# Attention scores of six chunks in 64x64 tiles of the array, with K loaded in interleaved groups of 64 tokens

## Chip, core and metric

The kernel runs on one core of a Trainium2 chip. The metric is the device time of one execution in microseconds (us). Its engines are named as in the profile: PE is TensorE (matmuls), PEld its weight loads, DVE is VectorE, ACT is ScalarE, POOL is GpSimd, and SP is SyncE, which here only issues DMAs.

## What is computed

Attention with 4 sink tokens and a sliding window of 128 tokens, for 4 batches, 8 heads, 768 tokens and a head size of 64, and then a feed-forward layer whose hidden value is the maximum of three products:

```python
scores = scale * np.matmul(q, k.transpose(0, 1, 3, 2))
is_sink = pos[None, :] < n_sink
rel = pos[:, None] - pos[None, :]
keep = is_sink | ((rel >= 0) & (rel < window))
scores = np.where(keep, scores, -1000000000.0)
a = np.exp(scores - max); a = a / (a.sum() + 1e-09)
x = np.matmul(a, v)          # heads side by side: 3072 tokens x 512
h = np.maximum(np.maximum(x @ w1, x @ w2), x @ w3)
out = h @ w_out
```

Inputs and output are float32; the kernel computes in bf16 with float32 sums.

## The kernel before

The tokens are cut into 12 chunks of 256, three to a batch (`CPB` = 3). A chunk has two blocks of 128 queries and two of 128 keys. Partitions hold pairs of tokens: in a load (`load`, L76) partition p holds tokens 2p and 2p+1 of the chunk, so a block n of 128 keys is on 64 partitions, with the two tokens of a pair (index i) side by side.

A chunk goes through these steps. POOL casts K, Q and V to bf16 (`cast_qk` L102, `cast_v` L108). For chunks 4 to 11 K and Q are turned by DMA transposes that SP issues (`turn_dma`, L153), K in two transposes of 64 partitions, Q in one. PE computes the scores of a pair of heads p (`score`, L272). The two heads (index a) of the pair are on partitions 0 to 63 and 64 to 127, so each matmul uses 64 rows of the array and all of its 128 columns. A chunk that is not the first of its batch has four score blocks of 128 keys by 128 queries: slot 0 is the block of the chunk before against the first queries, slots 1 and 2 the chunk's first keys against both query blocks, and slot 3 its second keys against the second queries. In each block a triangle lies outside the window, but all 128x128 are computed. ACT takes the exponential of a full PSUM bank per head (`expo`, L335), DVE multiplies by a mask of ones and zeros (`mask`, L341), and PE multiplies by V (`av`, L398) into four banks that `av_open` (L381) has started with the sink tokens. A first chunk of a batch (3, 6, 9) has three blocks per pair of heads and no sink part. From chunk 6 on these are packed into three sets of four (`score_packed` L307, `expo_packed` L318, `mask_packed` L323 with the mask `mskp`, which ACT copies from `msk0` during chunk 3, L221 to L224). The result x is turned by a DMA transpose (`xpose_dma`, L425), and PE runs the feed-forward layer: `ffn_h` (L438, nine groups of eight matmuls for a chunk, maxima on DVE at L449, first product copied by ACT at L445) and `ffn_y` (L459, twelve matmuls, copied out by DVE or ACT, L461).

All of this stands in an order that is written out by hand: each engine executes its instructions in the order of the program. From L715 on a loop runs over stages i = 3 to 11; stage i has the attention of chunk n = i + 1, the hidden layer of chunk i, the output layer of chunk m = i - 1, and loads, casts and transposes for chunk i + 3. In a stage the scores of pairs 0, 3 and 1 come first, then the twelve matmuls of `ffn_y`, then the scores of pair 2, and then `av` and `ffn_h` in turns. PSUM has eight banks; `bank` (L57) takes the bank that was given back longest ago and makes a new tile in it.

## Time and profile before

| | us |
|---|---|
| time, median of 3 runs | 177.45 (177.33 to 177.59) |
| the profiled execution | 177.2 |
| its span, first to last instruction | 175.4 |
| PE busy | 168.9 (96%), 1872 matmuls |
| DVE busy | 123.5 (70%) |
| ACT busy | 88.8 (51%) |
| POOL busy | 66.9 (38%) |

The profile is one execution. Its page gives busy times, a chain of waits (the work that ended last, followed back from the end) and groups of instructions by source line. Other views of the same trace are quoted with their filters named in words: a timeline gives start and duration in us, then engine, line, operation, tiles and, in brackets, the idle time before it and what ended it. Matmul ends are modelled, so a busy PE is not a PE at its peak, and start times say more than durations.

### The profile page before, as it was taken

How to read it: one execution, taken by the hardware profiler on the slowest of the kernel's cores; microseconds unless marked ns; L12 is line 12 of the kernel's file. 1: busy time of each engine (PE TensorE's matmuls, PEld its weight loads, DVE VectorE, ACT ScalarE, POOL GpSimd, SP SyncE). 2: the span in 40 equal slices, each digit the busy share in tenths (PEclk: the TensorE clock that was granted, in tenths of full speed). 3: DMA queues.
4: the chain of work that ended last, by engine and by line, in shares of the span. 5: the costliest groups of instructions: out<-in, count | busy, mean ns of one | idle time of the engine just before them, and what ended most of it. 6: DMA issues, size and time to landing. Idle time of an engine off the chain costs nothing.

```text
span 175.4 us, 4631 instructions
## 1 busy us (share of the span) xinstructions
PE 168.9 (96%) x1872; PEld 127.1 (72%) x1872; DVE 123.5 (70%) x264; ACT 88.8 (51%) x173; POOL 66.9 (38%) x123
## 2 busy tenths in 40 slices
PE   6989999999999999999999999999999999999991
PEld 2446889856896697697796796796895895896870
DVE  3389828599698496895875975877775775976460
ACT  3398741586995823814716715715517617510211
POOL 6785335046480555734735328038246000000000
PEclk9999999999999999999999999999999999999999
DMA  4999999994999989899999999999999429223203
GB/s 134 291 289 205 215 259 254 216 278 124 297 168 237 107 214 238 168 294 150 214 305 162 260 278 149 274 247 142 274 271 125 149 51 398 95 54 129 120 2 120
DMA packets 69573, 34.90 MB, mean 199 GB/s; under 512 B 26544, under 2 KB 68016, under 8 KB 69552
## 3 DMA queue, kind: packets, MB, share of 16 engines
q1 hardware_dynamic: 64912, 31.33, 80.0%
q0 software_dynamic: 4496, 3.15, 11.8%
q8 instruction: 14, 0.23, 0.6%
q10 hardware_dynamic: 144, 0.13, 0.2%
q14 instruction: 7, 0.06, 0.1%
HBM read 25.17 MB, written 6.29 MB: 179 GB/s over the span
## 4 chain that ended last, share of the span: by engine, by line
PE 90%; DMA 4%; SPq 2%; POOL 1%; issue 0%; DVE 0%; ACT 0%; POOLq 0%
PE h_ps L438 54%; PE y_ps L459 18%; PE o L398 6%; PE st L287 6%; DMA q_raw<-in_q_dram 4%; SPq L90 2%; PE xt L419 1%; PE o L381 1%; PE pt L118 1%; PE sk L349 1%; PE st L307 1%; PE y_ps L469 1%; POOL q_bf L102 1%; PE st L269 0%; PE pt L140 0%
## 5 line engine op out<-in xcount | busy, mean ns | idle before, releaser
L438 PE MATMUL h_ps<-xT,w 128*128 128x256 bf16 x864 | 100.4, 273 | 0.0
L438 PEld LDWEIGHTS <-w 128*128 128x128 bf16 x864 | 82.2, 98 | 10.2 <-issue 0.5
L449 DVE TENSOR_TENSOR h_sb<-h_sb,h_ps 128x512 bf16<-128x512 bf16 (+1 forms) x74 | 49.2, 671 | 20.3 <-PE h_ps L438 19.1
L445 ACT CAST h_sb<-h_ps 128x512 bf16<-128x512 f32 x36 | 21.2, 590 | 42.9 <-PE h_ps L438 42.9
L335 ACT ACTIVATE e_sb<-st 128x512 bf16<-128x512 f32 (+1 forms) x80 | 40.2, 593 | 1.0 <-PE st L287 0.8
L108 POOL CAST vb<-v_raw 64x512 bf16<-64x512 f32 x38 | 27.4, 722 | 15.6 <-DMA v_raw<-in_v_dram 10.7
L459 PE MATMUL y_ps<-wo,h_sb 128*128 128x512 bf16 x138 | 32.2, 380 | 0.0
L341 DVE TENSOR_TENSOR e_sb<-e_sb,msk 128x1024 bf16<-128x1024 bf16 (+1 forms) x34 | 24.9, 765 | 3.5 <-ACT e_sb L335 3.3
L459 PEld LDWEIGHTS <-h_sb 128*128 128x128 bf16 x138 | 12.6, 98 | 14.8 <-issue 1.2
L406 DVE TENSOR_TENSOR x_sb<-o,rc 128x256 bf16<-128x256 f32 x48 | 20.4, 425 | 1.7
L102 POOL CAST k_bf<-k_raw 128x512 bf16<-128x512 f32 x17 | 10.3, 625 | 28.5 <-DMA k_raw<-in_k_dram 25.8
L102 POOL CAST q_bf<-q_raw 128x512 bf16<-128x512 f32 x21 | 13.3, 659 | 14.9 <-DMA q_raw<-in_q_dram 11.4
L461 DVE COPY y_sb<-y_ps 128x512 f32<-128x512 f32 x13 | 9.0, 690 | 10.9 <-PE y_ps L459 10.8
L398 PE MATMUL o<-vb,e_sb 128*128 128x65 bf16 x352 | 16.4, 193 | 0.0
L398 PEld LDWEIGHTS <-e_sb 128*128 128x128 bf16 x352 | 14.6, 97 | 2.3
L287 PE MATMUL st<-qT,kT 64*128 64x128 bf16 (+1 forms) x224 | 12.5, 237 | 0.5 <-ACT kT L125 0.5
L287 PEld LDWEIGHTS <-kT 64*128 64x128 bf16 x224 | 7.1, 94 | 6.0 <-issue 3.8
L355 ACT ACTIVATE e_sink<-sk 128x256 bf16<-128x256 f32 x8 | 3.1, 386 | 15.0 <-PE sk L349 10.5
L403 DVE RECIPROCAL rc<-o 128x4 f32<-128x4 f32 x48 | 8.4, 176 | 3.2 <-PE o L398 3.1
L318 ACT ACTIVATE e_sb<-st 128x512 bf16<-128x512 f32 x12 | 6.1, 613 | 4.7 <-PE st L307 4.7
L461 ACT COPY y_sb<-y_ps 128x512 f32<-128x512 f32 x10 | 5.9, 588 | 2.1 <-PE y_ps L459 1.6
L102 ACT CAST k_bf<-k_raw 128x512 bf16<-128x512 f32 x5 | 3.1, 627 | 6.7 <-DMA k_raw<-in_k_dram 6.7
(78 smaller groups left out, 87.6 us busy)
## 6 DMA issues: line engine op xcount, KB each, us to landing
k_raw<-in_k_dram SPq DMA_DIRECT2D x12, 512.0 KB, 5.7
q_raw<-in_q_dram SPq DMA_DIRECT2D x12, 512.0 KB, 6.8
v_raw<-in_v_dram SPq DMA_DIRECT2D x12, 512.0 KB, 8.1
out_dram<-y_sb SPq DMA_DIRECT2D x11, 512.0 KB, 4.1
w<-in_moe_w_dram POOLq DMA_DIRECT2D x5, 256.0 KB, 8.6
w<-in_moe_w_dram POOLq DMA_DIRECT2D x2, 512.0 KB, 9.8
wo<-in_moe_w_out_dram POOLq DMA_DIRECT2D x2, 384.0 KB, 9.7
kT<-k_bf SPq DMA_TRANSPOSE x16, 3.5
```

The source lines that it names most:

```text
L102: f(x[:, 2 * g:2 * g + 2].rearrange("q p i a d -> q p a i d"), y[:, 4 * g:4 * g + 4].rearrange("q (p a) i d -> q p a i d", a=2))
L108: (eng.copy if eng is nc.scalar else eng.tensor_copy)(vb[ci % RING][64 * i:64 * i + 64, n, :, 0:D], raws[ci, "v"][64 * n:64 * n + 64, :, i])
L287: nc.tensor.matmul(st[a][:, s:s + q1 - q0].rearrange("q n (i r) -> q n i r", i=2), lhsT=x[hp, n, p].rearrange("q i r -> q (i r)"), rhs=qc[ ...
L335: nc.scalar.activation(e[:, a, lo:], st[a][:, lo:], AF.Exp, scale=scale)
L341: (eng or nc.vector).tensor_mul(e[:, :, lo:], e[:, :, lo:], msk0 if lo else msk)
L398: nc.tensor.matmul(o[:, t, a], lhsT=weight(ci, p, a, s), rhs=vb[cv % RING][:, n, 2 * p + a], start=first, stop=True, skip_group_check=True)
L406: nc.vector.tensor_mul(xs[ci][:, :, p], o[:, :, :, 0:D], rc.unsqueeze(3).to_broadcast([128, 2, 2, D]))
L438: nc.tensor.matmul(hp[:, f].rearrange("q (i t r) -> q i t r", i=2, t=2), lhsT=w_sb[wi][:, ds, c0:c0 + 128], rhs=xTs[ci][:, :, ds].rearrang ...
L445: nc.scalar.copy(dst, hp)
L449: nc.vector.tensor_max(dst[:, x], dst[:, x], hp[:, x])
L459: nc.tensor.matmul(yp, lhsT=hs[ci][:, fb, t * 128:(t + 1) * 128], rhs=wo[:, fb], start=(fb == 0), stop=(fb == FB - 1))
L461: (nc.scalar.copy if eng is None else eng.tensor_copy)(ys[ci][:, t], yp)
```

## The change

For chunks 6 to 11 (`SKEW` = 6) the 256 tokens of K and V are no longer taken as two blocks of 128 but as four groups g of 64 keys.

- K is loaded by four DMAs, one for each group, each onto every fourth partition (group g on partitions g, g+4, ...). After one transpose of all 128 partitions, the keys of a group stand four elements apart, and the matmul reads 64 of them as weights with a stride of four (`groups`).
- `score_skew` replaces `score`: 16 matmuls for a pair of heads instead of 6, each on 64 rows and 64 columns of the array (`tile_position=(64 * a, 64 * h)`, h = g % 2). Per head and column half it streams 128, 128, 64 and 64 query columns, where `score` streamed 128, 256 and 128 through all columns. Parts of the bank that no query needs are not written, and hold what was there before.
- `score_packed` of chunks 6 and 9 gives each of its matmuls to two 64-column tiles, with the same query columns: 32 matmuls instead of 16.
- Since the exponential may now read anything in the unwritten parts, the mask is a minimum with 0 or a very large number (`mskg`, `mskg0`, `mskp`) instead of a product. `mskg` is made by POOL behind K's cast for chunk 2; `mskg0` by POOL, and from it `mskp` by ACT, in stage 4 (the attention of chunk 5).
- V follows the groups' partition order: eight casts of 32 partitions instead of four of 64.
- `bank` makes eight tiles once and hands out views of them. Matmuls no longer wait on PE's own semaphore when a bank is taken again (93 such waits before); ACT's and DVE's reads of a bank name both PE and the other reader.

The core of the diff:

```diff
+        BANK = [psum.tile([128, 512], F32, name=f"bank{j}") for j in range(8)]
         def bank(shape, dtype, name):
             j = free.pop(0)
-            x = psum.tile(shape, dtype, tag=f"b{j}", name=name)
+            x = BANK[j][:, 0:n] if dtype is F32 else BANK[j][:, 0:n // 2].bitcast(dtype)
...
+        def groups(ci):
+            return kT[ci % RING].rearrange("q n p i r -> q (n p i r)").rearrange(
+                "q (p x g) -> q p x g", p=NP, g=4)
...
+                if w == "k" and ci >= SKEW:
+                    for g in range(4):
+                        nc.sync.dma_start(
+                            out=dst[g:128:4],
+                            in_=src[b, :, t0 + 64 * g:t0 + 64 * g + 64].rearrange("h (p i) d -> p h (i d)", i=2))
+                    continue
...
+            for h in range(2):
+                f(vb[ci % RING][64 * h + 32 * i:64 * h + 32 * i + 32, n, :, 0:D],
+                  raws[ci, "v"][64 * n + 32 * h:64 * n + 32 * h + 32, :, i])
...
+            if ci >= SKEW:
+                nc.sync.dma_start_transpose(
+                    out=groups(ci).rearrange("q p (i u) g -> q (p i) (u g)", i=2),
+                    in_=bfs[ci, w].rearrange("s p i a d -> s (p i a d)"))
+                return
...
+        def score_skew(ci, pairs):
+            k0, k1 = groups(ci - 1), groups(ci)
+            plan = ((1, k1, 0, 0, None), (2, k1, 1, 1, None), (3, k1, 2, 1, None), (0, k0, 3, 0, None),
+                    (2, k1, 0, 1, 0), (1, k1, 1, 0, 1), (0, k0, 2, 0, 0), (3, k1, 3, 1, 1))
+            for p in pairs:
+                st = [bank([128, 4, 128], F32, "st") for a in range(2)]
+                for s, x, g, t, u in plan:
+                    h = g % 2
+                    r = slice(0, 64) if u is None else slice(32 * u, 32 * u + 32)
+                    for a in range(2):
+                        hp = slice(64 * a, 64 * a + 64)
+                        nc.tensor.matmul(
+                            st[a][64 * h:64 * h + 64, s].rearrange("q (i r) -> q i r", i=2)[:, :, r],
+                            lhsT=x[hp, p, :, g],
+                            rhs=qT[ci % RING][hp, p, :, t, r],
+                            start=True, stop=True, tile_position=(64 * a, 64 * h))
...
-            nc.vector.tensor_mul(e, e, mskp[:, j // 2])
+            nc.vector.tensor_tensor(out=e, in0=e, in1=mskp[:, j // 2], op=ALU.min)
...
+                masks_skew(2) if i == 4 else None
...
+                masks_packed() if i == 4 else None
```

The order of instructions at three places. First PE, at the scores of the first pair of heads of chunk 8; `kT0` holds chunk 8's keys and `kT3` chunk 7's. Before, the whole pair:

```order
L287 LDWEIGHTS kT3_72
L287 MATMUL st_2102<-qT0_73,kT3_72 128x128
L287 LDWEIGHTS kT3_72
L287 MATMUL st_2103<-qT0_73,kT3_72 128x128
L287 LDWEIGHTS kT0_69
L287 MATMUL st_2102<-qT0_73,kT0_69 128x256
L287 LDWEIGHTS kT0_69
L287 MATMUL st_2103<-qT0_73,kT0_69 128x256
L287 LDWEIGHTS kT0_69
L287 MATMUL st_2102<-qT0_73,kT0_69 128x128
L287 LDWEIGHTS kT0_69
L287 MATMUL st_2103<-qT0_73,kT0_69 128x128
```

The middle of the same pair after the change, the second half of the long matmuls' last round and the first round of short ones:

```order
L348 LDWEIGHTS kT3_80
L348 MATMUL bank5_74<-qT0_81,kT3_80 64x128
L348 LDWEIGHTS kT3_80
L348 MATMUL bank2_71<-qT0_81,kT3_80 64x128
L348 LDWEIGHTS kT0_77
L348 MATMUL bank5_74<-qT0_81,kT0_77 64x2x32
L348 LDWEIGHTS kT0_77
L348 MATMUL bank2_71<-qT0_81,kT0_77 64x2x32
L348 LDWEIGHTS kT0_77
L348 MATMUL bank5_74<-qT0_81,kT0_77 64x2x32
L348 LDWEIGHTS kT0_77
L348 MATMUL bank2_71<-qT0_81,kT0_77 64x2x32
```

Three pairs of a weight load and a matmul per head have become eight, still with the two heads in turn, and four matmuls in a row now fall on four different tiles.

Second POOL, from the casts for chunk 6 to those for chunk 7 (`vb_87` and `vb_79` are chunk 6's V, `mskg_111` is `mskg0`). Before:

```order
L102 CAST q_bf<-q_raw 128x2x2x2x64 x2
L108 CAST vb_79<-v_raw 64x8x64 x4
L102 CAST k_bf<-k_raw 128x2x2x2x64 x2
L102 CAST q_bf<-q_raw 128x2x2x2x64 x2
L108 CAST vb_80<-v_raw 64x8x64 x4
L242 COPY ks_81<-kT_71 64x4x4 x2
```

After:

```order
L122 CAST q_bf<-q_raw 128x2x2x2x64 x2
L134 CAST vb_87<-v_raw 32x8x64 x8
L275 COPY mskg_111<-mskg 128x384
L277 MEMSET mskg_111 2x256 x2
L275 COPY mskg_111<-mskg 128x384
L277 MEMSET mskg_111 2x256 x2
L122 CAST k_bf<-k_raw 128x2x2x2x64 x2
L122 CAST q_bf<-q_raw 128x2x2x2x64 x2
L134 CAST vb_88<-v_raw 32x8x64 x8
L306 COPY ks_89<-kT_79 64x4x4 x2
```

V's casts have doubled, and six instructions for `mskg0` have come in ahead of chunk 7's casts.

Third ACT, between the hidden layer of stage 4 and the exponentials of chunk 6. Before, these stood behind one another:

```order
L445 CAST h_sb<-h_ps 128x512 x3
L318 ACTIVATE e_sb<-st 128x512 x6
L461 COPY y_sb<-y_ps 128x512
L445 CAST h_sb<-h_ps 128x512 x3
L355 ACTIVATE e_sink<-sk 128x256
```

After:

```order
L535 CAST h_sb<-bank_71 128x512
L283 COPY mskp<-mskg_111 128x2x384
L284 COPY mskp<-mskg_111 128x2x128
L286 COPY mskp<-mskg_111 128x2x256 x2
L405 ACTIVATE e_sb<-bank_70 128x512
L405 ACTIVATE e_sb<-bank_73 128x512
```

The four copies that make `mskp` have moved here from chunk 3's stage, and the first of them waits for POOL's `mskg0`.

83 lines of the change are left out of this document (66 added, 17 removed).

## Prediction

> **What bounds the kernel now.** I read the busy times first, then the chain of waits, by line and then in order of time.
>
> ```profile
> PE 168.9 (96%) x1872; PEld 127.1 (72%) x1872; DVE 123.5 (70%) x264; ACT 88.8 (51%) x173; POOL 66.9 (38%) x123
> PE 90%; DMA 4%; SPq 2%; POOL 1%; issue 0%; DVE 0%; ACT 0%; POOLq 0%
> ```
>
> PE's 96% alone proves little, since matmul ends are modelled. The chain says more: 90% of it is PE, unbroken but for 0.03 us from 13.60 us (the first row below) to the last output copy. There PE waits for nobody, so a nanosecond taken from its instructions is a nanosecond of the kernel, and work on other engines costs nothing until it makes PE wait. The stage with the attention of chunk 8 shows what a chunk's scores cost, and the rest that I need:
>
> ```profile
> 13.60 0.40 PE pt L140 x4
> ...
> 106.77 0.22 PE sk L349 x4
> 107.00 0.77 PE st L287 x18
> 107.77 2.70 PE y_ps L459 x12
> 110.46 0.33 PE st L287 x6
> 110.79 0.22 PE o L381 x8
> 111.01 0.35 PE o L398 x8
> 115.58 4.37 PE h_ps L438 x40
> 119.95 0.77 PE st L307 x16
> ```
>
> Three pairs of heads take 0.77 us and one takes 0.33, so a pair costs 0.22 and going into and out of the tiled mode 0.11. A matmul of `ffn_h` with 256 columns takes 4.37 / 40 = 0.109 us. A pair of heads streams 512 columns for each of two heads; at that pace one head alone is 0.218 us. So the two row halves of the array run side by side, and the scores are bound by streamed columns. The changed scores cost PE 4 x 1.10 = 4.4 us in chunks 7, 8, 10 and 11, and 2 x 0.77 in the packed chunks 6 and 9: the change works on 6 of 177 us.
>
> **The full chunks' scores.** A column half of a head now streams 128 + 128 + 64 + 64 = 384 columns. If all four tiles run side by side, as the two row halves do, a pair loses 128 columns, 128 x 0.109 / 256 = 0.055 us, and 16 pairs lose 0.87 us. Whether column tiles overlap and reload behind one another is shown by the sink rows, which use four tiles of 32 columns:
>
> ```profile
> 57.27 0.25 PE L365 MATMUL sv<-vb,sel 128*32 128x65 bf16 x8
> 57.34 0.28 PE L349 MATMUL sk<-qT,ks 128*32 128x256 bf16 x4
> 57.56 0.61 PE L459 MATMUL y_ps<-wo,h_sb 128*128 128x512 bf16 x2
> L349 PE MATMUL sk<-qT,ks x16: 270/283/283, 57.3 to 106.7; 128*32 128x256 bf16 x16
> ```
>
> Eight matmuls of 65 columns, each with weights of its own, pass in 0.07 us, two rounds of four; one after another they would need 8 x 65 x 0.109 / 256 = 0.22. So four column tiles overlap, and the second round's weights arrive within a round of 65 columns. The weights of the changed scores have 64 columns and a stride of four; no row has either. Between bounds of 0 (no gain, if each short round waits for its weights as long as a long one lasts) and -0.87 I take the whole -0.87, because the nearest rows are at that end.
>
> The first weights after a change of mode can't hide. In the last row the shortest of 16 matmuls (270 ns, the case in which other sink matmuls ran ahead) and the usual one (283) differ by 13 ns, which I read as one exposed load of 32 columns. Twice the columns make it 13 ns more, at eight entries in full chunks and two in packed ones: +0.13 us.
>
> **The packed chunks.** 32 matmuls for 16, with the same columns for each tile: 0 if the tiles overlap.
>
> Here the Trainium skill speaks against the change. Its page "TensorEngine Tiling (Array Packing)" (Restrictions and Gotchas) says that column tiling excludes the fast weight load, and "TensorE: Matmul & The Clock Gate" (LDWEIGHTS) puts a plain load at columns / 1.2 ns, which would be an estimated 53 ns for 64 columns, as long as a 128-column round; a pair would then save next to nothing. The 13 ns above for 32 columns is half of what that rule gives (27 ns), so I side with the row and keep the rule's result as a rival.
>
> **DVE, POOL and DMA, hidden.** The minimum takes the place of a product with the same operands, types and shape; no row has a minimum out of SBUF, I take 0, and the maximum of L449 bounds it from above (686 ns for half the elements, 0.6 us more per mask).
>
> V's casts double, since a cast costs by its row length:
>
> ```profile
> L108 POOL CAST vb<-v_raw 64x512 bf16<-64x512 f32 x38 | 27.4, 722 | 15.6 <-DMA v_raw<-in_v_dram 10.7 <-PE st L307 2.3 <-PE st L287 0.7
> 71.13 3.67 POOL L108 CAST vb<-v_raw 64x512 bf16<-64x512 f32 x4 [1.86 <-DMA v_raw<-in_v_dram]
> 77.09 1.17 POOL L102 CAST k_bf<-k_raw 128x512 bf16<-128x512 f32 x2 [2.30 <-DMA k_raw<-in_k_dram]
> 103.06 1.17 POOL L102 CAST k_bf<-k_raw 128x512 bf16<-128x512 f32 x2 [5.13 <-DMA k_raw<-in_k_dram]
> ```
>
> Four more at 0.72 are 2.9 us in a stage of 13 us, in which POOL idles 2 to 5 us ahead of the next K cast alone. Longer casts meet DVE's masks, which slow down beside POOL, but that has been paid already in chunk 5:
>
> ```profile
> 71.23 3.08 DVE L341 TENSOR_TENSOR e_sb<-e_sb,msk 128x1024 bf16<-128x1024 bf16 x3
> 109.81 1.92 DVE L341 TENSOR_TENSOR e_sb<-e_sb,msk 128x1024 bf16<-128x1024 bf16 x3
> 68.19:81.38 13.19, 13.19 (x154) 9.93 (x156) 10.30 (x19) 6.69 (x13) 6.92 (x10) 1.00 1.22 206
> 106.77:119.95 13.18, 13.18 (x155) 9.99 (x156) 9.31 (x19) 6.69 (x13) 4.97 (x9) 1.00 1.03 229
> ```
>
> Three masks took 3.08 us beside casts and 1.92 without, and the two stages are 13.19 and 13.18 us long: 0. K's four DMAs for one and one transpose for two change landing times by a microsecond or so, behind which q and v loads queue on SP; chunk 9's K, cast at 103.06, is first multiplied at 119.95, so 0, as long as the delay stays far below 10 us. The masks made early stand on POOL ahead of chunk 2's V casts:
>
> ```profile
> L198 POOL TENSOR_SCALAR_AFFINE_SELECT addm<-addm 64x128 bf16<-64x128 bf16 x2 | 0.6, 294 | 0.1
> 34.94 0.61 POOL L108 CAST vb<-v_raw 64x512 bf16<-64x512 f32 x1 [4.81 <-DMA v_raw<-in_v_dram]
> ```
>
> A memset, eight selects at 0.29 and a few copies are some 4 us, in the 4.81 in which POOL waits for that V: 0. The bank views take 93 waits of PE on itself away; forty matmuls of `ffn_h` in a row, with five new banks, already run at the 0.109 us of their columns, so there is nothing in them to gain: 0.
>
> **One place is tight: `mskp` for chunk 6.**
>
> ```profile
> L215 POOL TENSOR_SCALAR msk<-addm 128x384 bf16<-128x384 bf16 x2 | 1.1, 538 | 0.1
> L195 POOL MEMSET addm<- 128x256 bf16 x1 | 0.3, 318 | 0.0
> L221 ACT COPY mskp<-msk 128x768 bf16<-128x768 bf16 x1 | 0.8, 833 | 0.0
> L224 ACT COPY mskp<-msk 128x512 bf16<-128x512 bf16 x2 | 1.1, 616 | 0.0
> L222 ACT COPY mskp<-msk 128x256 bf16<-128x256 bf16 x1 | 0.4, 401 | 0.0
> 78.80 0.59 ACT L445 CAST h_sb<-h_ps 128x512 bf16<-128x512 f32 x1 [3.65 <-PE h_ps L438]
> 81.74 3.05 ACT L318 ACTIVATE e_sb<-st 128x512 bf16<-128x512 f32 x6 [2.36 <-PE st L307]
> 82.86 0.69 DVE L323 TENSOR_TENSOR e_sb<-e_sb,mskp 128x1024 bf16<-128x1024 bf16 x1 [0.75 <-ACT e_sb L318]
> 84.84 0.18 PE o L398 x6
> ```
>
> Chunk 6's V casts end at 74.8 now; four more end at 77.8. `mskg0` is two copies like L215 and four memsets like L195, 2.3 us: 80.1. ACT's copies are 0.83 + 0.40 + 2 x 0.62 = 2.5 us: 82.6, where the exponentials began at 81.74. They, and the six queued behind (DVE's first packed mask waits for them, and the copy of y behind it), start 0.9 us late; the mask, over at 83.55, ends at 84.4, and PE wants it at 84.7 to 84.8. That fits by 0.3 us. If K's four DMAs bring V a microsecond later, PE waits 0.7. I take 0.15.
>
> **Sum.** -0.87 + 0.13 + 0.15 = -0.59 us. The profiled execution is 177.2, so 176.6; the median of 177.45 is 0.25 above it, so **176.9** beside the runs.
>
> **Rivals.** *Slower: PE gets its instructions too slowly.* A load and its matmul go by every 0.22 / 6 = 37 ns now, and would have to every 10 ns.
>
> ```profile
> 17.84 0.22 PE o L381 x8
> 18.06 0.88 PE o L398 x24
> L307 PEldq EVENT_SEMAPHORE  x2: 51/51/51, 79.3 to 117.8; - x2
> ```
>
> The densest long stretch of the trace has 32 in 1.10 us, 34 ns each. PE's sequencer runs ahead: its wait for L307 stands at 117.8, 2 us before the first of these matmuls, so about 2 / 0.109 = 18 are ready. Of three pairs of heads, 48, some 30 come at 34 ns: 1.02 us for 0.66 in each of four chunks, +1.44; the last pair still saves 0.055 x 4, and 32 packed ones fit. With the 0.28 above this is +1.5, **179.0**. It turns against the change when a pair comes slower than 0.66 / 30 = 22 ns. Against it: 12 sink pairs in 0.29 us (57.27 to 57.56), though these fit into what is ready. The Trainium skill's "Runtime: NRT & Kernel Launch" (Instruction fetch mechanics) gives some 20 cycles for an instruction, an estimated 33 ns for a load and matmul; no run here shows it.
>
> *No gain: weights of 64 columns with a stride take as long as 128 streamed columns.* A pair stays at 0.22, and 0.28 is left: **177.7**.
>
> *The column halves don't overlap.* 768 columns for a pair, 0.33 us: +0.11 x 16 + 2 x 0.66 + 0.28 = +3.3, **180.8**; the sink rows speak against it.
>
> *Chunk 6 waits for its mask by 0.7 us:* **177.4**.
>
> **Chances.** Forecast 0.54 (176.5 to 177.2), instructions too slow 0.21, weights too slow 0.13, late mask 0.06, halves in turn 0.06. A difference under 0.2% (0.35 us) can't be told from none here. Faster 0.50, all of the forecast but its upper end; same 0.17 (0.04 of the forecast, 0.09 of the weights, 0.04 of the mask); slower 0.33. The range goes from 176.4, all of the columns' gain and no wait, to 179.1, which takes in the instruction case; the halves in turn are left out.
>
> **What would show it.** Eighteen changed score matmuls became 48: their piece of the chain in chunk 8 should fall from 0.77 to about 0.63 us, and the last pair's from 0.33 to 0.29. Pieces over 0.8 speak for slow instructions, of about 0.77 for slow weights, near 1.1 with packed pieces doubled for halves in turn. In chunk 6 no wait of PE on DVE should exceed 0.3 us. The stages of chunks 1 to 5 should keep their lengths; if they don't, the bank views did something that I cost at nothing.

## The result, and the profile after

The changed kernel takes 179.29 us (median of 4 runs, 179.19 to 179.50) against 177.52 us for the kernel before (4 runs), a ratio of 1.0101, 95% interval [1.0084, 1.0119]: slower by 1.0%. The forecast of 176.9 us was wrong, and its range ended at 179.1. Measured again (experiment 5) the ratio was 1.0076 [1.0054, 1.0098]. Beside experiments 1 to 4 the executions of the kernel before spread from 177.06 to 178.80 us, so one execution proves little, and the experiments below count more than one profile. Executions more than 1.5% above the fastest of their kernel are left out of the ratios but not of the medians, so the two need not agree.

In the page after, PE's share of the span is the same 96%, but its share of the chain has fallen from 90% to 87%, and DVE has come in with 5%. DMA's 4% was a load of the start-up; its 3% is now a transpose of x in the middle of the kernel:

```profile
PE 169.6 (96%) x2052; PEld 129.5 (73%) x2064; DVE 124.6 (70%) x264; ACT 88.7 (50%) x173; POOL 92.1 (52%) x167
...
PE 87%; DVE 5%; DMA 3%; issue 1%; ACT 1%; POOL 1%; POOLq 0%; DVEq 0%; ACTq 0%
```

PE's tiles are all named `bank` now, and lines have moved: `score_skew` is L348, `score_packed` L394, `ffn_h` L528. In the chain of waits of the changed kernel (start, us, what) the scores of chunk 8 and of the packed chunk 9 are longer than before, not shorter (0.77, 0.33 and 0.77; where a row has x15 for 16 matmuls, a record is missing from the trace):

```profile
108.89 0.85 PE bank L348 x48
...
112.44 0.37 PE bank L348 x15
...
121.97 0.83 PE bank L394 x32
```

A pair of heads takes (0.85 - 0.37) / 2 = 0.24 us where 0.22 stood and 0.165 was forecast. Further up, the same chain leaves PE in stage 4 for the transposed x and in chunk 6 for its mask (and once more ahead of both, along DVE from 36.3 to 40.5 us; experiment 13 comes back to that):

```profile
68.25 5.87 DMA xT<-x_sb
...
74.16 1.91 PE bank L528 x16
...
82.94 0.70 DVE h_sb L539
...
83.69 0.12 ACT mskp L286
...
84.21 1.08 ACT e_sb L405 x2
...
85.31 0.69 DVE e_sb L410
86.01 0.61 DVE y_sb L551
...
86.66 1.91 PE bank L528 x16
```

The matmuls of 86.66 started at 85.03 before. What releases them is the copy of y, which DVE makes behind the mask and which gives back a bank. Before the change that copy was early enough:

```profile
83.58 0.69 DVE L461 COPY y_sb<-y_ps 128x512 f32<-128x512 f32 x1
```

What comes ahead of `mskp` is on POOL and ACT. POOL's rows in the timeline of the changed kernel:

```profile
73.18 6.37 POOL L134 CAST vb<-v_raw 32x512 bf16<-32x512 f32 x8 [0.71 <-DMA v_raw<-in_v_dram]
79.62 0.50 POOL L275 COPY mskg<-mskg 128x384 bf16<-128x384 bf16 x1
...
81.45 0.64 POOL L277 MEMSET mskg<- 2x256 bf16 x2
```

ACT's rows:

```profile
82.12 0.83 ACT L283 COPY mskp<-mskg 128x768 bf16<-128x768 bf16 x1 [1.21 <-POOL mskg L277]
...
83.17 1.13 ACT L286 COPY mskp<-mskg 128x512 bf16<-128x512 bf16 x2
```

Chunk 6's V casts begin at 73.18, not at 71.13 as before; 0.92 of these 2.05 us is what the whole kernel was late by at this point (the table below), and the other 1.13 arise on SP's queue. Its rows of stage 3 in the timeline before:

```profile
60.35 1.23 SPq L157 DMA_TRANSPOSE qT<-q_bf  x1
61.63 0.58 SPq L90 DMA_DIRECT2D k_raw<-in_k_dram  x1
...
62.98 0.56 SPq L90 DMA_DIRECT2D v_raw<-in_v_dram  x1
66.26 1.79 SPq L425 DMA_TRANSPOSE xT<-x_sb  x1
```

And after:

```profile
62.25 1.23 SPq L182 DMA_TRANSPOSE qT<-q_bf  x1
63.53 2.70 SPq L105 DMA_DIRECT2D k_raw<-in_k_dram  x4
...
66.98 1.17 SPq L110 DMA_DIRECT2D v_raw<-in_v_dram  x1
68.25 3.25 SPq L515 DMA_TRANSPOSE xT<-x_sb  x1
```

K's four loads hold SP for 2.70 us instead of 0.58, and Q, V and the transpose of x stand behind them. In this execution SP also came to them later, by 1.90 us: the transpose of chunk 5's q ahead of them waited for its cast, 1 us longer than the kernel's shift explains. Before the change SP was idle for 2.7 us ahead of x's transpose; here it was not.

To see where time is lost, the table gives the start of the same `ffn_h` matmul in each kernel, minus its start before (us). The columns are places by the time in the kernel before: after the start-up, behind chunk 2's attention, ahead of and behind the first matmul that needs stage 4's x, behind chunk 6's mask, behind chunk 7, and the end.

| kernel | 21.4 | 45.7 | 66.7 | 72.6 | 84.9 | 98.0 | 168.7 | median, its before | ratio [95%] |
|---|---|---|---|---|---|---|---|---|---|
| changed | 0.45 | 0.92 | 0.92 | 1.55 | 1.80 | 1.90 | 2.31 | 179.29, 177.52 | 1.0101 [1.0084, 1.0119] |
| e5_again | 0.79 | 1.14 | 1.14 | 1.32 | 1.94 | 2.04 | 2.45 | 179.04, 177.69 | 1.0076 [1.0054, 1.0098] |
| e1_unit_stride | 0.77 | 1.05 | 1.05 | 1.31 | 1.94 | 1.89 | 1.56 | 177.89, 177.59 | 1.0005 [0.9978, 1.0032] |
| e2_views_only | 0.02 | 0.14 | 0.27 | 0.27 | 0.26 | 0.26 | 0.27 | 178.02, 177.59 | 1.0009 [0.9986, 1.0032] |
| e3_old_scores | 0.76 | 1.10 | 1.10 | 1.31 | 1.92 | 1.92 | 2.02 | 178.17, 177.59 | 1.0025 [0.9998, 1.0052] |
| e4_late_masks | 0.87 | 1.33 | 1.33 | 1.33 | 6.13 | 7.33 | 7.74 | 185.12, 177.59 | 1.0420 [1.0379, 1.0461] |
| e6_early_mskg0 | -0.03 | 0.02 | 0.03 | 0.83 | 0.88 | 0.97 | 1.40 | 178.00, 177.69 | 1.0018 [1.0002, 1.0033] |
| e9_strides | 0.04 | 0.14 | 0.27 | 0.44 | 0.48 | 0.57 | 1.56 | 178.45 (one run), 177.60 | |
| e10_kplain_early | 0.00 | 0.04 | 0.16 | 0.16 | 0.21 | 0.30 | 0.72 | 177.98, 177.60 | 1.0004 [0.9976, 1.0032] |
| e11_unit_early | 0.23 | 0.28 | 0.40 | 0.48 | 1.22 | 1.18 | 0.84 | 177.75 (one run), 177.60 | |
| e16_unit_kplain_early | 0.07 | 0.55 | 0.55 | 0.55 | 0.54 | 0.50 | 0.17 | 177.13, 177.55 | 0.9976 [0.9957, 0.9995] |
| e12_natural | 0.00 | 0.14 | 0.27 | 0.27 | 0.26 | 0.22 | 0.91 | 177.56, 177.60 | 0.9995 [0.9973, 1.0018] |
| e17_pairs | 0.05 | 0.08 | 0.21 | 0.21 | 0.21 | 1.36 | 1.04 | 179.87, 177.85 | 1.0084 [1.0049, 1.0119] |

The execution of the kernel before that is behind all these differences took 177.2 us, near the low end of its spread.

### The profile page after: what moved, and what is told of

Read it like the earlier page. It is cut to its first block, busy times and chain, and to the rows that moved or that the text cites. A ratio compares the mean times of both kernels' runs of the same rounds, so it can differ in the third digit from the quotient of the medians.

```text
span 177.5 us, 5117 instructions
## 1 busy us (share of the span) xinstructions
PE 169.6 (96%) x2052; PEld 129.5 (73%) x2064; DVE 124.6 (70%) x264; ACT 88.7 (50%) x173; POOL 92.1 (52%) x167
## 4 chain that ended last, share of the span: by engine, by line
PE 87%; DVE 5%; DMA 3%; issue 1%; ACT 1%; POOL 1%; POOLq 0%; DVEq 0%; ACTq 0%
PE bank L528 53%; PE bank L549 13%; PE bank L488 6%; DMA xT<-x_sb 3%; PE bank L373 3%; PE bank L348 3%; PE bank L333 2%; PE bank L210 2%; PE bank L143 1%; DVE h_sb L539 1%; PE bank L509 1%; DVE e_sb L431 1%; PE bank L439 1%; PE bank L471 1%; PE bank L559 1%
## 5 line engine op out<-in xcount | busy, mean ns | idle before, releaser
L528 PE MATMUL bank<-xT,w 128*128 128x256 bf16 x864 | 100.4, 273 | 0.5 <-DMA xT<-x_sb 0.5
L528 PEld LDWEIGHTS <-w 128*128 128x128 bf16 x864 | 82.3, 98 | 10.8 <-issue 1.0
L539 DVE TENSOR_TENSOR h_sb<-h_sb,bank 128x512 bf16<-128x512 bf16 (+1 forms) x74 | 49.1, 671 | 20.1 <-PE bank L528 18.5
L535 ACT CAST h_sb<-bank 128x512 bf16<-128x512 f32 x36 | 21.2, 588 | 43.1 <-PE bank L528 43.0
L422 ACT ACTIVATE e_sb<-bank 128x512 bf16<-128x512 f32 (+1 forms) x80 | 40.1, 589 | 1.1 <-PE bank L348 0.5
L134 POOL CAST vb<-v_raw 32x512 bf16<-32x512 f32 x48 | 37.6, 783 | 5.3 <-DMA v_raw<-in_v_dram 2.9
L549 PE MATMUL bank<-wo,h_sb 128*128 128x512 bf16 x126 | 31.1, 380 | 0.7 <-issue 0.2
L496 DVE TENSOR_TENSOR x_sb<-bank,rc 128x256 bf16<-128x256 f32 x48 | 20.4, 424 | 1.6
L488 PE MATMUL bank<-vb,e_sb 128*128 128x65 bf16 x352 | 16.3, 193 | 0.3 <-DVE e_sb L431 0.3
L429 DVE TENSOR_TENSOR e_sb<-e_sb,mskg 128x1024 bf16<-128x1024 bf16 x16 | 13.3, 866 | 0.0
L130 POOL CAST vb<-v_raw 64x512 bf16<-64x512 f32 x14 | 9.8, 703 | 3.2 <-DMA v_raw<-in_v_dram 2.7
```

The source lines that it names most:

```text
L134: f(vb[ci % RING][64 * h + 32 * i:64 * h + 32 * i + 32, n, :, 0:D], raws[ci, "v"][64 * n + 32 * h:64 * n + 32 * h + 32, :, i])
L422: nc.scalar.activation(e[:, a, lo:], st[a][:, lo:], AF.Exp, scale=scale)
L429: nc.vector.tensor_tensor(out=e[:, :, lo:], in0=e[:, :, lo:], in1=mskg, op=ALU.min)
L488: nc.tensor.matmul(o[:, t, a], lhsT=weight(ci, p, a, s), rhs=vb[cv % RING][:, n, 2 * p + a], start=first, stop=True, skip_group_check=True)
L496: nc.vector.tensor_mul(xs[ci][:, :, p], o[:, :, :, 0:D], rc.unsqueeze(3).to_broadcast([128, 2, 2, D]))
L528: nc.tensor.matmul(hp[:, f].rearrange("q (i t r) -> q i t r", i=2, t=2), lhsT=w_sb[wi][:, ds, c0:c0 + 128], rhs=xTs[ci][:, :, ds].rearrang ...
```

## Experiments

**1. The stride.** The same kernel with neighbouring columns as weights:

```diff
-                            lhsT=x[hp, p, :, g],
+                            lhsT=x[hp, p, 64 * g:64 * g + 64],
```

> The changed kernel with one difference: the 64-column weights of the scores of chunks 6 to 11 are read with unit stride (64 neighbouring columns of kT) instead of a stride of four. That pairs the wrong keys with the masks, so the scores are not the reference's; instructions, sizes and everything else are the same. In the changed kernel a pair of heads came every 240 ns, four rounds of four tiles at 60 ns. Theory 1 (a load of 64 columns into a column tile takes some 60 ns, whatever its stride): a pair stays at 240 ns, the first piece of chunk 8 stays at about 0.85 us, the time stays at 179.3 within 0.3. Theory 2 (the stride of four slows the load): a pair falls towards its 384 streamed columns, 164 to 175 ns, the piece to about 0.65, and the kernel by 16 x 0.065 = 1.0 us to about 178.2.

Measured in its chain of waits:

```profile
95.66 0.86 PE bank L352 x46
...
99.21 0.30 PE bank L352 x16
...
108.89 0.65 PE bank L352 x48
...
112.23 0.30 PE bank L352 x16
```

0.65 and 0.30, so a pair takes 0.175 us, and theory 2 holds: column tiles of 64 overlap and their loads hide; the stride of four does not. The view by source shows the loads (ns min/median/max) of the changed kernel:

```profile
L348 PEld LDWEIGHTS <-kT x256: 131/142/156, 95.4 to 151.4; 64*64 64x64 bf16 x128
```

And of this one:

```profile
L352 PEld LDWEIGHTS <-kT x256: 102/107/111, 95.6 to 150.7; 64*64 64x64 bf16 x128
```

But chunk 7 keeps its 0.86 us for three pairs. Its third pair needs a bank that DVE gives back when it has taken the last maximum of the hidden layer, at 96.10:

```profile
94.61 1.49 DVE L543 TENSOR_TENSOR h_sb<-h_sb,bank 128x512 bf16<-128x512 bf16 x2 [0.26 <-PE bank L532]
```

The table shows it: the shift falls by 0.05 us in chunk 7, and from 84.9 us to the end by 0.38.

**2. Bank views alone**, in the kernel before:

```diff
+        BANK = [psum.tile([128, 512], F32, name=f"bank{j}") for j in range(8)]
-            x = psum.tile(shape, dtype, tag=f"b{j}", name=name)
+            x = BANK[j][:, 0:n] if dtype is F32 else BANK[j][:, 0:n // 2].bitcast(dtype)
```

> The kernel before with one part of the change alone: the eight tiles BANK with views handed out of them. Nothing else is changed. In the changed kernel the start-up up to the first 80 h matmuls was 0.45 us later than before, and another 0.45 us came in the stretch of chunks 2 and 3 (33 to 41 us). Theory 1 (the views' waits cost the start-up): the 80 h matmuls start at 21.9 instead of 21.5, and the kernel takes 178.0 (178.4 if the second 0.45 is theirs too). Theory 2 (the start-up differs by something else, such as the layout of the program or the landing of the first loads): 177.5, no difference, h at 21.5.

The start-up shift is 0.02: the views did not cause it. A further 0.25 appears up to 67 us; e10 shows 0.16 there and e6 0.03 with the same views, so it can't be told from what executions differ by.

**3. Scores in the old form**, all else changed:

```diff
-                for s, x, g, t, u in plan:
+                for s, x, n, q0, q1 in ((0, k0, 1, 0, 1), (1, k1, 0, 0, 2), (3, k1, 1, 1, 2)):
...
-                            lhsT=x[hp, p, :, g],
+                            lhsT=x[hp, p, 128 * n:128 * n + 128],
```

> The changed kernel with the scores of chunks 6 to 11 as matmuls of the form before: six of 128 columns for a pair of heads and 16 in a packed chunk, with 128 neighbouring columns of kT as weights, so that the keys are in the wrong order. All else of the change stays: loads, one transpose, V's casts, masks, bank views. What it lacks against the changed kernel is the price of the tiled scores. Theory 1 (tiled scores cost 0.02 us a pair and 0.06 a packed chunk, and the other parts the remaining 1.2 us): 178.8, with stages of 13.1 to 13.2 us from chunk 7 on, and the shifts before chunk 6 unchanged. Theory 2 (the longer stages from chunk 7 on come from V's doubled casts and their contention, not from the scores): 179.3.

From behind chunk 6 on the shift grows by 0.10 us to the end, against 0.51 in the changed kernel: the strided scores cost about 0.4 us more than the old ones, and V's casts lengthen no later stage. Theory 1, though the time, 178.17 us, is less than its 178.8.

**4. The early masks moved behind chunk 6's casts:**

```diff
-        masks_skew(0)
-        masks_skew(1)
         cast_v(2, 0, 1, nc.gpsimd)
...
                 cast_v(i + 3, 1, 1, nc.gpsimd)
+                masks_skew(0)
+                masks_skew(1)
```

> The changed kernel with POOL's instructions for mskg and selg moved: from ahead of chunk 2's V casts to behind chunk 6's casts in stage 3, where they are still ready before chunk 6. Theory 1 (these some 4 us of POOL work delay chunk 2's V casts and slow DVE beside them, and so cost the 0.45 us between 33 and 41 us): y x6 of stage 1 at 40.5 instead of 41.0 us, and 178.85. Theory 2 (the 0.45 comes from the bank views or elsewhere): 179.3 and y at 41.0.

Neither theory. The shift behind chunk 2 is 1.33, so these instructions cost nothing early; but the place I moved them to was not free, since `mskg0` stands behind them. The chain runs along POOL and ACT into PE:

```profile
85.95 0.31 POOL mskg L277
...
87.43 1.04 ACT mskp L286 x2
88.46 0.99 ACT e_sb L405 x2
...
91.00 3.01 PE bank L528 x16
```

PE's matmuls that stood at 86.66 start at 91.00, later by 4.3 us, the length of the moved work (79.58 to 83.8 us on POOL): chunk 6's wait is POOL's chain. The next 16 matmuls took 3.01 us instead of 1.91; PE had waited 4.19 us ahead of them, and its granted clock from 90.4 to 94.0 us was 0.60.

**5. The changed kernel once more.**

> The changed kernel itself, unchanged, once more, so that its start-up can be set beside the other executions. In the six executions seen so far the nine warm matmuls at 4.8 us change from 427 to 216 ns each at moments between 4.6 us and 8.0 us. Theory 1 (that moment is not the program's): it falls at another moment here than 7.1 us, and the 80 h matmuls start later or earlier than 21.96 us by the same; the runs spread over more than 1 us, as those of the kernel before did on the last chip, and the difference in medians to the kernel before stays 1.5 to 2 us. Theory 2 (bank views or another part of the change put it there): it stays at 7.1 us and the h matmuls at 21.96.

The nine warm matmuls of the start-up, in the timeline (start, us) of the kernel before:

```profile
4.84 2.45 PE L180 MATMUL warm<-wz 128*128 128x512 bf16 x9
```

The changed kernel:

```profile
4.91 3.20 PE L210 MATMUL bank<-wz 128*128 128x512 bf16 x9
```

This run:

```profile
4.90 3.55 PE L210 MATMUL bank<-wz 128*128 128x512 bf16 x9
```

And e6, below:

```profile
4.90 2.25 PE L210 MATMUL bank<-wz 128*128 128x512 bf16 x9
```

The same program takes 3.20 and 3.55 us for them, and e6, which differs only far behind, 2.25. The moment at which they double their pace belongs to the execution; so does the start-up shift, 0.45 and 0.79 us in these two and 0.77 and 0.23 in e1 and e11, which are one program as well. Theory 1. The ratio fell to 1.0076, a difference of 1.35 us, less than the 1.5 to 2 expected.

**6. Chunk 6's mask made in stage 3:**

```diff
                 turn_dma(i + 2, 'k')
+                masks_skew(2)
...
+                masks_packed()
                 xpose_dma(n)
...
-                masks_skew(2) if i == 4 else None
-                masks_packed() if i == 4 else None
```

> The changed kernel with the making of chunk 6's mask put earlier: POOL's six instructions for mskg0 from behind chunk 6's V casts in stage 4 to stage 3, ahead of chunk 5's q casts, and ACT's four copies to mskp to the end of stage 3. Everything else as changed. Theory 1 (the chain V casts, mskg0, mskp, exponentials, mask, y copy holds PE in chunk 6): the shift against the kernel before no longer grows at chunk 6 (it grew by 0.3 to 0.6 us there), and the kernel gains 0.3 to 0.6 us against the changed one. Theory 2 (chunk 6 waits for its V or K anyway, which K's four loads make late): the shift grows at chunk 6 as much as before, 0 gain.

The median falls from e5's 179.04 to 178.00, more than expected, and the shift grows at chunk 6 by 0.05 instead of 0.62: theory 1. But in this profile x came later instead:

```profile
67.45 5.95 DMA xT<-x_sb
```

So from 66.7 to 84.9 us it lost 0.85 us, as much as the changed kernel (0.88). Its whole lead over the profile of e5, 1.05 us at the end, lies ahead of 66.7 us; that the 1.04 us between the medians are all the mask's is therefore not shown.

**7 and 8. Another layout of K**, with one load and four short transposes (8 with the early mask too):

```diff
+                for g in range(4):
+                    nc.sync.dma_start_transpose(
+                        out=flat(ci)[:, g].rearrange("q p i u -> q (p i) u"),
+                        in_=bfs[ci, w][32 * g:32 * g + 32].rearrange("s p i a d -> s (p i a d)"))
```

> The changed kernel with another layout of K: one plain load as before the change, and four transposes of 32 partitions, one for each group of 64 tokens, in place of one of 128, so that a group's 64 columns are neighbours and the scores' weights are read with unit stride. All else as changed; it computes the reference. Theory 1 (stride of four slowed the weights; K's four loads made the chunk after late): a pair comes every 175 ns, 0.65 us for chunk 8's first piece, and the shift in chunks 4 to 6 no longer grows by the waits for xT and V: 177.8 to 178.3 at a start-up like the kernel before's. Theory 2 (four short transposes take the DMA queues and SP as long as the four loads did): the pieces are the same 0.65, but PE waits in stages 3 and 4 as in the changed kernel, 178.5 or more.

> The two edits together: K by one plain load and four transposes with unit stride for the weights, and mskg0 and mskp made in stage 3. All else as changed; it computes the reference. If both causes are right and nothing else is late, what is left of the change is its gain: 0.05 us for each of 8 pairs of heads in chunks 8 and 11 and less in 7 and 10, where the third pair waits for a bank, so about -0.5 us: 177.0 where the kernel before has 177.5. If V's doubled casts or DVE's minimum cost something of their own, it stays at or above the kernel before.

188.33 us (1.0612 [1.0576, 1.0648]) and 188.99 (1.0540 [1.0504, 1.0575]), far from both theories. From stage 6 on x lands late, as the chain of 7 says (of an execution of 190.74 us):

```profile
94.67 7.60 DMA xT<-x_sb
```

Its list of DMA issues (count, median us to landing):

```profile
kT<-k_bf SPq DMA_TRANSPOSE x28, 3.5
...
xT<-x_sb SPq DMA_TRANSPOSE x8, 7.2
```

In the changed kernel x took 4.4 us to land, with 10 transposes of K. Short transposes are no way out.

**9. Four other strides,** one for each full chunk:

```diff
+            st_w = {7: 4, 8: 2, 10: 3, 11: 8}[ci]
-                            lhsT=x[hp, p, :, g],
+                            lhsT=x[hp, 128 * p + g:128 * p + g + 63 * st_w + 1:st_w],
```

> The changed kernel with chunk 6's mask made early (as in the run of that name), and another stride of the 64-column weights in each full chunk: 4 in chunk 7, 2 in chunk 8, 3 in chunk 10, 8 in chunk 11, and 1 in the packed chunk 9. The keys are wrong but for chunk 7, so the scores are not the reference's. Read from the piece of the chain with the last pair of heads, 16 matmuls: 0.37 us at a stride of four and 0.30 at one in the runs so far (0.24 and 0.175 for a pair). Theory 1 (a load reads SBUF in lines of 16 bytes, and slows with the number of lines: 64 columns of two bytes at stride 1, 2, 3, 4, 8 are 8, 16, 24, 32, 64 lines): 2 is hidden or nearly (0.30 to 0.33), 3 in between, 4 at 0.37, 8 at 0.5 or more. Theory 2 (any stride but one takes the same slower path): 0.37 at 2, 3, 4 and 8.

Its chain, chunks 8, 10 and 11:

```profile
107.57 0.65 PE bank L352 x48
...
110.92 0.30 PE bank L352 x15
...
132.78 0.88 PE bank L352 x45
...
136.35 0.32 PE bank L352 x16
...
146.06 1.56 PE bank L352 x48
...
150.32 0.60 PE bank L352 x16
```

Last pairs: 0.30 at a stride of two, 0.32 at three, 0.37 at four (the changed kernel), 0.60 at eight. A pair at eight takes (1.56 - 0.60) / 2 = 0.48 us, 120 ns for each of its four rounds of four tiles; at four 60 ns; at two the load is hidden. From four to eight the time doubles, as the number of theory 1's lines does (32, 64), and the other strides lie in order, so theory 2 is out. That the unit is a line of 16 bytes is not shown: a time in proportion to a longer piece of memory fits these strides as well. The Trainium skill's "SBUF — State Buffer" (Door 1: The DMA port swizzle) speaks of such lines and lets bf16 stride by up to eight for free; these loads agree with the lines, not with eight: free up to two.

**10. One plain load of K**, early mask, stride of four:

```diff
-                if w == "k" and ci >= SKEW:
-                    for g in range(4):
...
-                    continue
```

> The changed kernel with chunk 6's mask made early and K of chunks 6 to 11 loaded by one plain DMA, as before the change, in place of four; the one transpose and the stride of four stay. The groups then hold the wrong keys, so the scores are not the reference's. Theory 1 (K's four loads, 0.61 us of SP's queue each, and what they do to the DMA queues, made the x transposes of stage 4 late, which cost 0.8 us with the early mask): no growth of the shift between 65 and 73 us, and 177.3 to 177.6 at an early start-up, 0.7 us under the run with the early mask alone. Theory 2 (the single transpose of 128 partitions or V's casts make xT late): the growth of 0.8 us stays.

No growth between 66.7 and 72.6, as in e2, e13 and e16, which load K plainly too; with K's four loads it was 0.00 (e4) to 0.80 (e6) in eight executions. But the median, 0.38 us above its before, is no better than e6's 0.31, while the ratio is, 1.0004 for 1.0018: what K's loads cost in the time once the mask is early can't be told from these. Half of theory 1.

SP's rows say why x waited so differently. In six of the eight executions SP still idled for 1.18 us ahead of x's transpose, and this landed 5.8 to 6.4 us after its issue, where it took 4.8 to 5.7 in the kernel before, e2, e10, e13 and e16: waits of 0.00 to 0.26 us. In the other two, changed and e6, chunk 5's q came 1 us late as well, SP had no idle time left, and x was issued 1.1 to 1.2 us late: waits of 0.63 and 0.80.

**11. Experiment 1 once more.**

> The changed kernel with unit stride for the weights (wrong keys, as in the first run of that name), mask as late as in the changed kernel; a second look at the same program. Both theories of the weights agree on the pieces (0.65 and 0.30). What it tells is the part of the 16 x 0.065 us that the kernel keeps: the first look kept 0.38 us over chunks 7 to 11, with the third pair of chunks 7 and 10 waiting 0.19 us for a bank that DVE's h copy gives back. Theory 1 (that wait follows from the faster scores): it is here again, in both chunks. Theory 2 (chance): in at most one of them.

0.86 us for three pairs in both chunk 7 and chunk 10, 0.65 in 8 and 11: theory 1, the wait for a bank follows from the faster scores. The mask was late again, and here the chain runs without a break from K's four loads through V, `mskg0` and the exponentials to the copy of y that PE waits for:

```profile
61.89 0.73 SPq L109
...
65.33 6.86 DMA v_raw<-in_v_dram
...
78.74 0.51 POOL mskg L279
...
83.42 0.99 ACT e_sb L409 x2
...
85.43 0.61 DVE y_sb L555
```

**12. K and V in another order of tokens**, K unit stride, two V casts:

```diff
-                if w == "k" and ci >= SKEW:
-                    for g in range(4):
+                if w != "q" and ci >= SKEW:
+                    for i in range(2):
                         nc.sync.dma_start(
+                            out=dst[:, :, i],
+                            in_=src[b, :, t0 + 128 * i:t0 + 128 * i + 128].rearrange("h p d -> p h d"))
```

> A version that may beat both, and computes the reference: K and V of chunks 6 to 11 are loaded with token p and token p + 128 on partition p, by two DMAs each with packets of 256 bytes instead of 512. Then one transpose puts a group's 64 keys on neighbouring columns, the weights have unit stride, V needs two casts of 128 partitions instead of eight of 32, and the masks two selects instead of eight; mskg0 and mskp are made early. Theory 1 (stride, K's four loads and the late mask were all that stood in the way): the pieces are 0.65 and 0.30, PE waits neither in stage 4 nor in chunk 6, and it gains 0.4 to 0.6 us on the kernel before: 177.0 where that has 177.5. Theory 2 (loads in packets of 256 bytes take longer than the slack): k_raw or v_raw land some us later, xT or V come late, and it is at or above the kernel before.

A tie. Up to chunk 9 its shift fell to 0.14; then, by its chain, x was late in stage 9:

```profile
131.62 6.00 DMA xT<-x_sb
```

**13. A late start forced on the kernel before** (`warm(14)` for `warm(9)`):

> The kernel before with 14 warm matmuls instead of nine ahead of chunk 0's transposes, so that PE's start-up is late by up to 5 x 0.216 = 1.1 us whenever the clock changes. Nothing else is changed. Theory 1 (the loss between 33 and 46 us follows a late start in any kernel): the shift grows there by another 0.3 to 0.5 us, as in the changed kernel. Theory 2 (it is the change's, by early masks or bank views): the shift stays as it was at 33 us.

Shift 0.67 at 21.4 us, 0.93 at 45.7, and 0.92 to the end. A loss of 0.26 us in that stretch needs nothing of the change. Nor does it need a late start: e16 lost 0.48 there with an early one. The traces show what goes with it. In the seven executions in which POOL was already casting q when DVE began the second of its two V casts there, that cast took 0.74 to 0.87 us and the stretch lost 0.26 to 0.48; in the other thirteen the cast took 0.43 us and the stretch lost at most 0.14. Theory 1 only in part.

**14 and 15. V's loads elsewhere** in the version of 12: on POOL's queue, or on SP behind the transposes.

```diff
-                        nc.sync.dma_start(
+                        (nc.gpsimd if w == "v" else nc.sync).dma_start(
```

```diff
-                load(i + 3)
+                load(i + 3, 'kq')
...
                 turn_dma(i + 3, 'q')
+                load(i + 3, 'v')
```

> The version with tokens p and p + 128 on a partition, with V's two loads issued by POOL's queue instead of SP's. It computes the reference. Theory 1 (SP's queue, in which V's loads stood ahead of the x transpose, cost the 0.93 us in stage 9): no wait for xT there, and 0.5 us under the kernel before. Theory 2 (the DMA engines themselves are full, 104% of a window's time with the small packets): xT waits as long, and the issues on POOL delay its casts besides: no better than that version, 177.6.

> The same version with V's loads moved behind the transposes of each stage on SP, and V's casts a stage later on POOL. It computes the reference. Theory 1 (order on SP): the x transpose of each stage is issued as soon as x is there, no wait for xT, and 0.5 us under the kernel before, 177.0 to 177.2. Theory 2 (full DMA engines): xT or the transposes of K and q land late in some other stage, 177.6 or more.

183.35 us (1.0324 [1.0293, 1.0355]) and 180.93 (1.0151 [1.0111, 1.0191]): x was late by more, in 14 in stages 6 and 9, in 15 in 8 and 9. Theory 2 is nearer both times, but x came later than it said, and that full DMA engines were the reason is not shown.

**16. The idea without the layout's costs:** one plain load of K, unit stride, early mask; the edits of 1, 6 and 10.

> The changed kernel with K by one plain load and one transpose, weights with unit stride and chunk 6's mask early; the keys are then in the wrong places, so the scores are not the reference's. V keeps its eight casts, the masks their minimum. It is what the change's idea would give if the layout cost nothing. Theory 1 (no other part of the change costs anything): the shift from chunk 7 on falls by 0.05 us in chunks 7 and 10 and 0.15 in 8 and 11, 0.4 in all, and it gains 0.2 to 0.4 us on the kernel before. Theory 2 (V's casts or the minimum cost something where nothing else hides them): less than 0.1 us gained.

177.13 against 177.55, ratio 0.9976 [0.9957, 0.9995]: the only kernel that beats the one before. From 84.9 us to the end its shift falls by 0.37 us. So nothing else of the change costs anything that shows: V's casts, the minimum and the views are in it. Its minimum takes 808 ns (16 masks), its products 804 (14).

**17 and 18. Two last layouts:** groups interleaved in pairs (stride of two, four loads, two transposes), and the version of 12 with two stores put off.

```diff
-                            out=dst[g:128:4],
+                            out=dst[64 * (g // 2) + g % 2:64 * (g // 2) + 64:2],
...
-                            lhsT=x[hp, p, :, g],
+                            lhsT=x[hp, g // 2, p, g % 2:128:2],
```

```diff
-                store(i - 4)
+                store(i - 4) if i < 8 else None
```

> A version that may beat both and computes the reference: K's groups are interleaved in pairs within each half of a chunk, by four loads as in the change, so that the weights have a stride of two (which was hidden in chunk 8 of the run with several strides); two transposes of 64 partitions as before the change; chunk 6's mask early; and chunk 6's four K loads issued ahead of the transpose of chunk 5's q, where SP waits for POOL for 3 us. Theory 1 (stride, SP's queue in stage 4 and the late mask were the three costs): pieces of 0.65 and 0.30, no wait for xT in stage 4, and 0.2 to 0.4 us under the kernel before, as the run with one plain load and wrong keys. Theory 2 (four loads and two transposes a stage are too much for SP in other stages too, now that nothing else is late): an x transpose late in one of stages 5 to 9 by 0.5 to 1 us, and a tie or slower.

> The version with tokens p and p + 128 on a partition, with the stores of two chunks of y (stages 8 and 9) put off to stage 10, behind its x transpose, and seven buffers for y instead of five. It computes the reference. Theory 1 (the store of 512 KB fills the DMA engines just when the loads and the x transpose of stage 9 need them): no wait for xT in stage 9, 0.3 to 0.5 us under the kernel before. Theory 2 (it is V's two issues on SP, which stand ahead of the x transpose whatever is stored): the wait of 0.9 us stays, and so does the tie.

179.87 us, and 178.03 against 177.85 (1.0012 [0.9987, 1.0038]). In 17 stage 4 waits no more, but stage 6 does, by 1.15 us (its chain):

```profile
91.92 7.42 DMA xT<-x_sb
```

In 18 x was late in stages 4, 6 and 9. No layout with the keys in their places beat the kernel before; e12 ties with it.

## Why the prediction was wrong, point by point

The medians make a ladder, each kernel against its before: changed +1.35 (e5), mask early +0.31 (e6), K loaded plainly +0.38 (e10), unit stride -0.42 (e16). Its steps depend on their order, and the intervals are 0.3 to 0.5 us wide to each side: by way of e1 (+0.30) the stride alone takes 1.05 us away, not 0.80, and mask and loads together 0.72, not 0.97.

The table separates the two better, because it compares places. From 84.9 us to the end the stride of four loses 0.51 to 0.52 us in four profiles (changed, e5, e6, e10) and unit stride gains 0.37 to 0.38 in three (e1, e11, e16), so the stride costs 0.9. From 66.7 to 84.9 us, in chunk 6's mask and stage 4's x, the late mask and K's four loads lose 0.80 to 0.89 in five profiles (changed, e1, e3, e5, e11). With the mask alone made early it was 0.21 and 0.85 (e9, e6), and with one plain load besides 0.05 and nothing (e10, e16). The two losses, 0.51 and some 0.85, match the 1.35 of the medians. How the second divides between the mask and the loads stays open: they are parts of one chain (e11), and a kernel with the late mask and one plain load, otherwise as changed, was not run.

- **PE is the bound.** Right, and it is why 0.02 us a pair comes through. But the chain may leave PE where another engine's slack ends, which it did in stage 4 and in chunk 6.
- **Scores of the full chunks, -0.87.** Wrong, in the step "the weights of the changed scores have 64 columns and a stride of four; no row has either [...] I take the whole -0.87, because the nearest rows are at that end". The sink rows have unit stride, so they were near in the columns and silent on the stride. With unit stride (e16) the five chunks behind chunk 6 gave -0.37: chunks 8 and 11 -0.15 each, where the forecast has four times 0.055 less twice 0.013, -0.19; chunks 7 and 10 gave -0.05, because their third pair now waits for a bank, a cost that the prediction has at nothing. With the stride of four the four full chunks cost +0.45. The exposed first load was sized right: entering and leaving took 0.30 - 0.175 = 0.125 us for a forecast of 0.11 + 0.013, with some luck, as the 13 ns were read from durations whose ends are modelled.
- **The rival of slow weights** had the right place, and 0.13 was too little; its lower bound, no gain, was still too good. Its reason was only half right: 64 columns in a column tile are no slower to load (a pair in 0.175 us has four rounds, 44 ns on average, where the rule of the Trainium skill's "TensorEngine Tiling (Array Packing)" and "TensorE: Matmul & The Clock Gate" that I set aside gives an estimated 53 each); the stride alone is.
- **Packed chunks, 0.** +0.06 each with the stride (0.83 for 0.77), and 0.02 or less without it (e16): the overlap was judged rightly.
- **K's four DMAs, 0.** The step that failed is "chunk 9's K, cast at 103.06, is first multiplied at 119.95, so 0". It asked who needs K and not who stands behind K on SP. The four issues held SP 2.1 us longer; V was cast 1.13 us later than the kernel's shift of 0.92 explains, and PE waited 0.63 us for the transposed x (0.00 to 0.80 in eight executions).
- **`mskp`'s chain, +0.15.** The chain was right, instruction by instruction: V's casts 6.37 us for 6.6, `mskg0` 2.5 for 2.3, `mskp` 2.2 for 2.5. But it began 1.13 us late against the rest of the kernel, which the prediction had named as what would break it ("If K's four DMAs bring V a microsecond later, PE waits 0.7"). And "That fits by 0.3 us" measured the slack at the mask. What PE waits for is the copy of y behind the mask: it ended at 84.27 before, and PE took the bank at 84.86 by the timeline, 85.03 by the chain. The 0.9 us that the prediction put on the mask would make that copy 0.1 to 0.3 us late even with V on time. Mis-sized: 0.25 us at the mask in the profile after, 0.60 to 0.74 in the four executions where x had waited less.
- **Early masks, V's casts, minimum, views: 0.** Right as far as it can be measured (e4, e3, e16, e2). The casts' 2.7 us more mattered only inside the chain above.
- **Stages of chunks 1 to 5 keep their lengths.** They didn't in the profile after, and the prediction would have blamed the views. It was the execution: start-up 0.45 us, and a like sum between 33 and 46 us, where two engines' casts met, as they did with the views and without them (e16, e13). The wait for x in stage 4 is the change's own, through SP's queue.

## What to carry to other kernels

Price weights that are read with a stride apart from their column count: here every second column was free, every fourth was not. Give the transpose a destination in which a tile's columns are neighbours. When a load is cut in four, count the issue time on its queue and walk down that queue to what stands behind it; the price is paid by the first of those that has no slack. Read an engine's slack at the last instruction that somebody waits for, not at the one that you changed. And a table that is needed once belongs where its engine is idle, not on the last stage before its use.

## What the runs showed of the hardware that I had not expected

- A load of 64 bf16 columns into each of four 64x64 tiles: hidden behind rounds that stream 64 and 128 columns at strides of one and two (44 ns a round on average), 60 ns a round at a stride of four, 120 at eight (e1, e9).
- The start-up's change of pace (427 to 216 ns for a matmul of 512 columns) fell at another moment in each execution; the nine warm matmuls took 2.25 to 3.55 us in the four shown. The Trainium skill's "TensorE: Matmul & The Clock Gate" (Part 1) puts it down to an activity window that runs freely and is not set back when a kernel starts, which agrees. So 0.45 us of a single profile's difference says nothing here.
- 28 transposes of K instead of 10, 24 of them of 32 partitions, took x's transpose from 4.4 to 7.2 us to landing and made the kernel 6% slower than the one before (e7).
- A PE that had waited 4.19 us in chunk 6 ran its next 16 matmuls in 3.01 us instead of 1.91, at a granted clock of 0.60 (e4).
- A V cast on DVE that began while POOL was casting q took 0.74 to 0.87 us instead of 0.43, in seven of twenty executions.
